# Softmax groups of eight heads instead of four, with the loads of keys and values reshaped to match, in a decode transformer block

## The chip, the cores and the metric

The kernel runs on 1 core of one Trainium2 chip. The metric is device time in microseconds (us) for one execution. The kernel before takes 189.02 us, the median of 3 runs (188.81 to 189.14).

## The reference

One decode step of a transformer block with adaptive layer norm, batch 2, one query token per batch entry. Attention over the last 1024 of 4096 cached tokens, then a gated FFN. Cut to the attention:

```python
B, Sq, D = 2, 1, 640
Hq = Hkv = 32; Sk = 4096; Dh = 192
W = 1024                                  # min(4096, max(256, Sk // 4))
q = (h @ wq).reshape(B, Sq, Hq, Dh).transpose(0, 2, 1, 3)
k = k_cache[:, :, Sk - W:, :]             # (B, 32, 1024, 192) bfloat16
v = v_cache[:, :, Sk - W:, :]
p = softmax(einsum('bhqd,bhkd->bhqk', q, k) * Dh ** -0.5)
o = einsum('bhqk,bhkd->bhqd', p, v)       # then @ wo, residual, layer norm, FFN
```

Keys and values are 50.3 MB of the 76.9 MB that have to be read (2 tensors x 2 batch entries x 32 heads x 1024 tokens x 192 x 2 bytes). The weights are the rest.

## The kernel before

K and V, the keys and values, are read from off-chip memory (HBM; the page counts 76.88 MB read from it) and pass through a ring of 8 slots in on-chip memory (SBUF, 128 partitions or "rows"). A slot holds one load: one contiguous run of 12288 B for each of the 128 rows, 1.57 MB. A group is four heads of one batch entry. Row 4p + i of a slot holds 32 neighbouring tokens, block p of 32, of head i of 4. DVE (VectorE) multiplies K by the query, PE (TensorE, the matmul engine) adds up over part of the head dimension, DVE finishes the scores, and one softmax chain per group follows (maximum, subtract, exp on ACT, which is ScalarE, denominator, probabilities times V or "PV", scaling).

```python
HQ = 4                      # heads in a group
PH = P // HQ                # 32 token blocks
J = W // PH                 # 32 tokens in each row
NG = B * NQD                # 16 groups
NS, SLOT = 8, J * Dh        # ring
# ... order of the loads: wq, k0, then k(g) and v(g-1) in turn, then wo
def ring_src(it):
    # ... wq and wo cut
    quad, b = group(i)
    src = A_k_cache if kind == "k" else A_v_cache
    return src[b].rearrange("(i u) s d -> u i s d", u=NQD)[quad, :, K0:Sk, :].rearrange("i (p j) d -> p i (j d)", p=PH), SLOT
# ... one DMA for each load, issued as soon as the slot's last user is known
S.dma("sp", k_dma(ring_f[:, o0:o0 + width], src), sem_ring[slot_of[it]], writes=ring_key(it), ...)
```

What the DMA instruction gets from this, in elements (step, count), outermost dimension first: source `[6144, 32] [6291456, 4] [1, 6144]`, destination `[49152, 128] [1, 1] [1, 6144]`. The text calls this shape 32 x 4: 32 blocks of 4 runs.

Of the kernel before, what the change touches and what calls it, by code (L numbers as in the profile page):

```python
# [5 lines left out]
ALU = mybir.AluOpType  # L6
ACTF = mybir.ActivationFunctionType
AX = mybir.AxisListType
BF16 = mybir.dt.bfloat16
# [110 lines left out]
def bass_adaLN_cond__sliding_block_cached__geglu_ffn__decode_kernel(  # L120
# [14 lines left out]
    P = 128  # L135
    B, _, D = A_x.shape
    _, H, Sk, Dh = A_k_cache.shape
    F = B_w_gate.shape[1]
    W = min(4096, max(256, Sk // 4))
    K0 = Sk - W  # L140
    KT = D // P
    NQ = H * Dh
    NR = 4
    DR = D // NR
    HQ = 4
    PH = P // HQ
    J = W // PH
    NQD = H // HQ
    NG = B * NQD
    NT = NQ // P  # L150
    DD = Dh // NT
# [3 lines left out]
    assert DD * NT == Dh and DD * H == P and NR * FR == FC and FC * P == F and DR == KT * 32  # L155
    assert HQ == NR and DD * NQD == 32
    SCALE = float(Dh) ** -0.5
    EPS = 1e-5
    NEG = 1e30
    JC = 16  # L160
    NCK = J // JC
    GC = 512 // JC
    NCH = Dh // GC
    assert GC * NCH == Dh and NCK == 2
    ON = 2 * Dh
    NPAIR = J // 2

    NS = 8
    SLOT = J * Dh
    WQ_SPLIT = [(0, 2), (2, 3)]  # L170
# [6 lines left out]
    HP = P // 2  # L177
    X0 = DD * NQD - 1
    ZW = X0 + P
    QW = 512  # L180
    NQB = NQ // (NR * QW)
    FT = F // NR
    assert NQB * QW == NQD * Dh
    MH = 3 * DR

    es = ExitStack()
    with es:
# [23 lines left out]
        selrow = sb("selrow", [P, NR, B], BF16)  # L211
        selq = sb("selq", [P, B, P], BF16)
        ztmp = sb("ztmp", [P, NR, 2, HQ], BF16)
# [39 lines left out]
        def bank(k):  # L253
            return ("bank", k)
# [13 lines left out]
        items = [("wq", k) for k in range(NWQ)]  # L268
        items += [("k", 0)]
        for g in range(1, NG):  # L270
            items += [("k", g), ("v", g - 1)]
        items += [("v", NG - 1)]
        items += [("wo", i) for i in range(NWO)]
# [18 lines left out]
        def group(g):  # L292
            return divmod(g, B)

        def ring_src(it):
            kind, i = it
            if kind == "wq":
                k0, n = WQ_SPLIT[i]
                return A_wq.rearrange("(p k) n -> p (k n)", k=KT)[:, k0 * NQ:(k0 + n) * NQ], n * NQ
            if kind == "wo":  # L300
                t0, n = WO_SPLIT[i]
                return A_wo.rearrange("(p t) n -> p (t n)", t=NT)[:, t0 * D:(t0 + n) * D], n * D
            quad, b = group(i)
            src = A_k_cache if kind == "k" else A_v_cache
            return src[b].rearrange("(i u) s d -> u i s d", u=NQD)[quad, :, K0:Sk, :].rearrange("i (p j) d -> p i (j d)", p=PH), SLOT

# [17 lines left out]
        for nm, t in (("scT", scT), ("oT", oT), ("aT", aT)):  # L324
# [15 lines left out]
                                                compare_op=ALU.is_equal, fill=0.0, base=0, channel_multiplier=1),  # L340
             reads=["ones_b"], writes=["selg"], name="selg")
        for b in range(B):
            S.op("pool", lambda e, b=b: e.affine_select(out=selq[:, b, :].rearrange("p (x h) -> p x h", h=HQ),
                                                        in_=ones_b[:, 0:1].unsqueeze(2).broadcast_to([P, PH, HQ]),
                                                        pattern=[[0, PH], [-32, HQ]],
                                                        compare_op=ALU.is_equal, fill=0.0, base=-b, channel_multiplier=1),
                 reads=["ones_b"], writes=[("selq", b)], name="selq%d" % b)
        S.op("pool", lambda e: e.affine_select(out=ztmp[:, :, :, :].rearrange("p i q h -> p i (q h)"),
# [61 lines left out]
        def ln_mod(tag, opc_idx, s_idx, dst_bf):  # L410
# [7 lines left out]
            def f(e):  # L418
                last = None
                hv = hrow[:, :].rearrange("p (m j) -> p m j", j=KT)  # L420
                for j in range(KT):
                    for i in range(NR):
# [10 lines left out]
             reads=["mask_h"], writes=["maskc"], name="maskc")  # L433
        S.op("dve", lambda e: e.tensor_reduce(out=zsel[:, :, X0:X0 + P].rearrange("p q (h m) -> p q h m", m=32)[:, :, :, 0],
                                              in_=ztmp[:, :, :, :].rearrange("p i q h -> p q h i"), axis=AX.X, op=ALU.max),
# [36 lines left out]
        for n in range(NQB):  # L472
# [3 lines left out]
            else:  # L476
                S.op("dve", lambda e, n=n: e.tensor_copy(out=qrow[:, n * QW:(n + 1) * QW], in_=ps[:, n, :]),  # L477
                     reads=[bank(n)], writes=[("qrow", n)], name="q1_evac%d" % n)
        for u, (n, b) in enumerate((n, b) for n in range(NQB) for b in range(B)):
            bk = BK_T + u % 4  # L480
            S.op("pe", lambda e, n=n, b=b, bk=bk: e.matmul(ps[:, bk, :], lhsT=selq[:, b, :], rhs=qrow[:, n * QW:(n + 1) * QW], start=True, stop=True),
                 reads=[("selq", b), ("qrow", n)], writes=[bank(bk)], name="q2_%d_%d" % (n, b))
            S.op("act", lambda e, n=n, b=b, bk=bk: e.activation(out=qbc[:, b, n * QW:(n + 1) * QW], in_=ps[:, bk, :], func=ACTF.Copy),  # L483
                 reads=[bank(bk)], writes=[("qbc", b, n)], name="q2_evac%d_%d" % (n, b))
        S.op("dve", lambda e: e.memset(ps[:, 5:8, :], 0.0), writes=[bank(k) for k in range(5, 8)], name="init_O2")  # L485

        def d_mul(g, ci):
            quad, b = group(g)
            sl = slot_of[("k", g)]
            S.op("dve", lambda e: e.tensor_tensor(out=prod[:, 2 * (g % 2) + ci, :, :],  # L490
                                                  in0=ring[:, sl, ci * JC * Dh:(ci + 1) * JC * Dh].rearrange("p (j d) -> p j d", d=Dh),
                                                  in1=qbc[:, b, quad * Dh:(quad + 1) * Dh].unsqueeze(1).broadcast_to([P, JC, Dh]), op=ALU.mult),
                 reads=[("ring", sl)] + [("qbc", b, n) for n in range(quad * Dh // QW, ((quad + 1) * Dh - 1) // QW + 1)], writes=[("prod", 2 * (g % 2) + ci)], name="mul%d_%d" % (g, ci))

        def p_reduce(g, ci):
            pz = 2 * (g % 2) + ci

            def f(e):
                last = None
                o_ap = ps[:, pz, :].rearrange("p (j c) -> p j c", c=GC)  # L500
                for t in range(NCH):
                    last = e.matmul(o_ap, lhsT=ident_b[:, :], rhs=prod[:, pz, :, t * GC:(t + 1) * GC],  # L502
                                    start=(t == 0), stop=(t == NCH - 1))
                return last
            S.op("pe", f, reads=[("prod", pz), "ident_b"], writes=[bank(pz)], name="red%d_%d" % (g, ci))

        def c_sum(g):
            z = g % 2
            S.op("dve", lambda e: e.tensor_reduce(out=S_sb[:, z, :], in_=ps[:, 2 * z:2 * z + 2, :].rearrange("p k (j c) -> p (k j) c", c=GC),  # L509
                                                  axis=AX.X, op=ALU.add),  # L510
                 reads=[bank(2 * z), bank(2 * z + 1)], writes=[("S", z)], name="sum_%d" % g)
            S.op("dve", lambda e: e.tensor_reduce(out=M1[:, z:z + 1], in_=S_sb[:, z, :], axis=AX.X, op=ALU.max),  # L512
                 reads=[("S", z)], writes=[("M1", z)], name="max_%d" % g)
            S.op("pe", lambda e: e.transpose(ps[0:1, BK_T, 0:P], M1[:, z:z + 1], ident_f[:, :]),
                 reads=[("M1", z), "ident_f"], writes=[bank(BK_T)], name="T_%d" % g)
# [26 lines left out]

        def p_pv(g):
            z = g % 2
            sl = slot_of[("v", g)]

            def f(e):
                last = None
                for jp in range(NPAIR):
                    i = jp % NR  # L550
                    last = e.matmul(ps[32 * i:32 * i + 2 * HQ, BK_O, 0:ON],  # L551
                                    lhsT=E_sb[:, z, 2 * jp:2 * jp + 2, :].rearrange("p j h -> p (j h)"),
                                    rhs=ring[:, sl, 2 * jp * Dh:(2 * jp + 2) * Dh],
                                    start=(jp < NR), stop=(jp >= NPAIR - NR), tile_position=(0, 32 * i))
                return last
            S.op("pe", f, reads=[("E", z), ("ring", sl)], writes=[bank(BK_O)], name="PV_%d" % g)

# [24 lines left out]

        for g in range(NG + 2):
            has = g < NG
            prev = 1 <= g <= NG
            pp = g >= 2
            if has:
                d_mul(g, 0)
                p_reduce(g, 0)
            if pp:  # L590
                c_rec(g - 2)
            if prev:
                c_sum(g - 1)
            if has:
                d_mul(g, 1)
                declare_ring([("k", g)])
            if prev:
                c_max2(g - 1)
                c_bc(g - 1)
            if has:  # L600
                p_reduce(g, 1)
            if prev:
                c_exp(g - 1)
                p_den(g - 1)
            if pp:
                p_sel(g - 2)
            if prev:
                p_pv(g - 1)
                declare_ring([("v", g - 1)])

# [119 lines left out]
```

## Time and profile before

| | before |
|---|---|
| time, median | 189.02 us |
| DMA rate, 60 to 140 us | 426 GB/s |
| DVE busy, PE busy, ACT busy | 98.2, 107.5, 29.9 us of a span of 187.6 |
| end of the last weight load | 184.4 us |

The first part of the page to read is the span in 40 slices. DMA is the mean busy share of the 16 DMA engines in tenths, and GB/s is what they moved:

```profile
DVE  6131100019588988886595695775865933003211
...
DMA  7999998999999999999999999999999999999991
GB/s 254 402 451 435 430 459 372 422 435 424 430 422 422 427 425 426 427 424 420 419 432 432 422 423 422 421 438 422 424 423 422 419 488 428 416 384 442 398 396 45
```

DMA is at 9 (90% or more) nearly from end to end, and after the start the rate is mostly between 415 and 440 GB/s. DVE has gaps. The same for one stretch (the last two columns are the DMA share and GB/s):

```profile
core 0: us, PE busy (x) PEld busy (x) DVE busy (x) ACT busy (x) POOL busy (x), PEclk, DMA share, GB/s
60.00:140.00 80.00, 54.89 (x440) 27.29 (x439) 61.19 (x83) 11.42 (x36) 0.00 (x0) 0.96 1.01 426
```

The list of DMA issues gives the kind of load, the count, the size and the median time from issue to landing:

```profile
ring<-in_A_k_cache_dram SPq DMA_DIRECT2D x16, 1536.0 KB, 24.4
ring<-in_A_v_cache_dram SPq DMA_DIRECT2D x16, 1536.0 KB, 24.2
```

One load takes 3.7 us at 426 GB/s, so 24 us mean that six or seven loads are queued. Last, what the main DVE step waited for (waits of all engines):

```profile
engine line waited for: us in total, times, longest us
...
DVE prod L490 <- DMA ring<-in_A_k_cache_dram: 14.3, 9, 1.6
```

The products wait 14.3 us in all for K. The kernel is bound by its loads. The chain that ended last says the same, in shares of the span by engine:

```profile
## 4 chain that ended last, share of the span: by engine, by line
DMA 71%; DVE 15%; PE 7%; ACT 2%; SPq 2%; issue 1%
```

### The profile page before, as it was taken

To read this page: it belongs to the slowest core of one execution; us is meant where nothing else is said; L and a number is where in the kernel's file an instruction comes from. 1 tells how busy PE (TensorE), PEld (TensorE's weight loads), DVE (VectorE), ACT (ScalarE), POOL (GpSimd) and SP (SyncE) were. 2 spreads that over 40 slices of the span, in tenths; PEclk is the share of its full clock that TensorE was granted. 3 is DMA by queue.
4 is the path that set the end of the run, shared out by engine and by line. 5 is a ranking of instruction groups with operands and counts; after the bars stand their busy time and mean duration, and the time that the engine had idled before them with its cause. 6 is when DMAs were issued, how large, how long until landed. Compare 5 with 4: busy or idle time off the path is not lost.

```text
span 187.6 us, 2409 instructions
## 1 busy us (share of the span) xinstructions
PE 107.5 (57%) x1039; PEld 51.1 (27%) x1039; DVE 98.2 (52%) x147; ACT 29.9 (16%) x72; POOL 5.1 (3%) x23
## 2 busy tenths in 40 slices
PE   0014730742968887676676655675497395364462
PEld 0011200210323443333423323233253152353121
DVE  6131100019588988886595695775865933003211
ACT  3041100082001221112011110210120103103400
POOL 8200000000000000000000000000000000000000
PEclk9999999997587999999879999999969967569696
DMA  7999998999999999999999999999999999999991
GB/s 254 402 451 435 430 459 372 422 435 424 430 422 422 427 425 426 427 424 420 419 432 432 422 423 422 421 438 422 424 423 422 419 488 428 416 384 442 398 396 45
DMA packets 6518, 77.03 MB, mean 411 GB/s; under 512 B 746, under 2 KB 876, under 8 KB 1516
## 3 DMA queue, kind: packets, MB, share of 16 engines
q1 hardware_dynamic: 6492, 76.88, 97.1%
q8 instruction: 8, 0.13, 0.3%
q10 hardware_dynamic: 16, 0.01, 0.0%
q14 instruction: 2, 0.02, 0.0%
HBM read 76.88 MB, written 0.00 MB: 410 GB/s over the span
## 4 chain that ended last, share of the span: by engine, by line
DMA 71%; DVE 15%; PE 7%; ACT 2%; SPq 2%; issue 1%
DMA ring<-in_A_k_cache_dram 37%; DMA ring<-in_A_wq_dram 17%; DMA r<-in_B_w_down_dram 17%; DVE prod L490 9%; PE ps L502 4%; DVE S_sb L509 4%; PE ps L467 2%; SPq L266 2%; ACT qbc L483 2%; DVE ps L485 1%; DVE M L512 1%; ACT qrow L474 1%; PE ps L526 0%; DVE bcR L519 0%; PE ps L684 0%
## 5 line engine op out<-in xcount | busy, mean ns | idle before, releaser
L490 DVE TENSOR_TENSOR prod<-ring,qbc 128x3072 bf16<-128x3072 bf16 x32 | 55.9, 1751 | 14.3 <-DMA ring<-in_A_k_cache_dram 14.3
L502 PE MATMUL ps<-prod,ident_b 128*128 128x512 bf16 x192 | 52.9, 419 | 14.4 <-DVE prod L490 14.4
L502 PEld LDWEIGHTS ps<-prod,ident_b 128*128 128x128 bf16 x192 | 17.5, 104 | 40.2 <-DVE prod L490 17.5
L509 DVE TENSOR_REDUCE S_sb<-ps 128x32 f32<-128x1024 f32 x16 | 19.3, 1206 | 2.1 <-PE ps L502 2.1
L526 PE MATMUL ps<-bcR,bcL 5*128 5x4 f32 x32 | 6.1, 258 | 21.9 <-DVE bcR L519 21.9
L563 ACT ACTIVATE On<-ps,rden 128x384 bf16<-128x384 f32 x16 | 9.3, 580 | 43.5 <-DVE rden L561 21.1
L551 PE MATMUL ps<-ring,E_sb 128*8 128x384 bf16 x256 | 15.5, 369 | 0.0
L534 ACT ACTIVATE E_sb<-Sb_sb 128x128 bf16<-128x128 f32 x16 | 5.0, 310 | 56.4 <-DVE Sb_sb L531 56.4
L467 PE MATMUL ps<-ring,hT 128*2 128x512 bf16 x60 | 6.7, 626 | 9.8 <-DMA ring<-in_A_wq_dram 8.8
L526 PEld LDWEIGHTS ps<-bcR,bcL 5*128 5x128 f32 x32 | 4.7, 183 | 26.1 <-DVE bcR L519 26.1
L477 DVE CAST qrow<-ps 128x512 bf16<-128x512 f32 x1 | 0.7, 692 | 15.7 <-PE ps L467 15.7
L622 PE MATMUL ps<-ring,oT 128*17 128x160 bf16 x192 | 5.5, 294 | 5.6 <-DMA ring<-in_A_wo_dram 5.6
L531 DVE TENSOR_TENSOR Sb_sb<-S_sb,ps 128x128 f32<-128x128 f32 x16 | 4.6, 287 | 7.6 <-PE ps L526 7.6
L540 PEld LDWEIGHTS ps<-denp,maskc 128*128 128x128 f32 x32 | 7.1, 224 | 3.7 <-ACT E_sb L534 0.9
L641 DVE TENSOR_TENSOR lnt<-ps,modR 128x160 f32<-128x160 f32 x1 | 0.3, 325 | 12.6 <-PE ps L622 12.6
L445 PE MATMUL ps<-r,scT 128*17 128x480 bf16 x40 | 4.3, 597 | 3.9 <-DMA r<-in_w_mod_dram 3.9
L622 PEld LDWEIGHTS ps<-ring,oT 128*17 128x17 bf16 x192 | 4.9, 117 | 6.2 <-DMA ring<-in_A_wo_dram 6.2
L551 PEld LDWEIGHTS ps<-ring,E_sb 128*8 128x8 bf16 x256 | 5.1, 90 | 3.7 <-issue 1.2
L396 PE MATMUL ps<-st,selstat 128*128 128x2 f32 x4 | 0.9, 298 | 8.6 <-ACT sqj L392 8.6
L467 PEld LDWEIGHTS ps<-ring,hT 128*2 128x2 bf16 x60 | 1.7, 114 | 14.7 <-DMA ring<-in_A_wq_dram 9.7
L576 PE MATMUL ps<-On,zsel 128*128 128x96 bf16 x64 | 5.2, 241 | 0.7 <-ACT On L563 0.7
L540 PE MATMUL ps<-denp,maskc 128*128 128x1 f32 x32 | 5.1, 230 | 0.8 <-ACT E_sb L534 0.8
(81 smaller groups left out, 71.2 us busy)
## 6 DMA issues: line engine op xcount, KB each, us to landing
ring<-in_A_k_cache_dram SPq DMA_DIRECT2D x16, 1536.0 KB, 24.4
ring<-in_A_v_cache_dram SPq DMA_DIRECT2D x16, 1536.0 KB, 24.2
r<-in_w_mod_dram SPq DMA_DIRECT2D x1, 4800.0 KB, 14.3
ring<-in_A_wq_dram SPq DMA_DIRECT2D x1, 4608.0 KB, 32.3
ring<-in_A_wo_dram SPq DMA_DIRECT2D x1, 4480.0 KB, 23.4
ring<-in_A_wq_dram SPq DMA_DIRECT2D x1, 3072.0 KB, 21.2
ring<-in_A_wo_dram SPq DMA_DIRECT2D x1, 2720.0 KB, 24.1
r<-in_B_w_gate_dram SPq DMA_DIRECT2D x1, 1920.0 KB, 25.0
```

Source lines behind the costliest of these rows:

```text
L467: last = e.matmul(ps[32 * i:32 * i + B, n, :], lhsT=hT[:, k, :], rhs=wv[:, kk, i, n * QW:(n + 1) * QW], start=(k == 0), stop=(k == KT - 1) ...
L490: S.op("dve", lambda e: e.tensor_tensor(out=prod[:, 2 * (g % 2) + ci, :, :], in0=ring[:, sl, ci * JC * Dh:(ci + 1) * JC * Dh].rearrange("p ...
L502: last = e.matmul(o_ap, lhsT=ident_b[:, :], rhs=prod[:, pz, :, t * GC:(t + 1) * GC], start=(t == 0), stop=(t == NCH - 1))
L509: S.op("dve", lambda e: e.tensor_reduce(out=S_sb[:, z, :], in_=ps[:, 2 * z:2 * z + 2, :].rearrange("p k (j c) -> p (k j) c", c=GC), axis=A ...
L526: S.op("pe", lambda e: e.matmul(ps[:, BK_T, P:P + HQ], lhsT=bcL[:, :], rhs=bcR[:, z, :], start=True, stop=True), reads=[("bcR", z), "bcL"] ...
L531: S.op("dve", lambda e: e.tensor_tensor(out=Sb_sb[:, z, :, :], in0=S_sb[:, z, :].unsqueeze(2).broadcast_to([P, J, HQ]), in1=ps[:, BK_T, P: ...
L534: S.op("act", lambda e: e.activation(out=E_sb[:, z, :, :], in_=Sb_sb[:, z, :, :], func=ACTF.Exp, scale=SCALE, accum_out=denp[:, z:z + 1]), ...
L540: S.op("pe", lambda e: e.matmul(ps[:, BK_T, P + 16:P + 17], lhsT=maskc[:, :], rhs=denp[:, z:z + 1], start=True, stop=True), reads=[("denp" ...
L551: last = e.matmul(ps[32 * i:32 * i + 2 * HQ, BK_O, 0:ON], lhsT=E_sb[:, z, 2 * jp:2 * jp + 2, :].rearrange("p j h -> p (j h)"), rhs=ring[:, ...
L563: S.op("act", lambda e: e.activation(out=On[:, quad % 2, b, :], in_=ps[:, BK_O, 0:ON], func=ACTF.Identity, scale=rden[:, z:z + 1]), reads= ...
L576: last = e.matmul(ps[:, BK_OT, 0:B * NT].rearrange("p (b t) -> p b t", b=B), lhsT=zsel[:, jj, x:x + P], rhs=On[:, quad % 2, :, jj * Dh + d ...
L622: last = e.matmul(ps[32 * i:32 * i + RM, BK_M, 0:DR], lhsT=oT[:, t, :], rhs=wv[:, tl, i, :], start=(t == 0), stop=(t == NT - 1), tile_posi ...
```

## The change

Its intent is to halve the number of softmax chains: groups of eight heads, 8 groups instead of 16. Eight heads on 128 rows leave 16 token blocks of 64 tokens. So that a slot keeps its size, each K or V of a group comes as two loads, each with half of every block's 64 tokens.

```diff
-    HQ = 4
+    HQ = 8
+    V = HQ // NR
+    JS = 32
+    NSUB = J // JS
...
-    SLOT = J * Dh
+    SLOT = JS * Dh
...
-        items += [("k", 0)]
-        for g in range(1, NG):
-            items += [("k", g), ("v", g - 1)]
-        items += [("v", NG - 1)]
+        items += [("k", sq) for sq in range(NSUB)]
+        for sq in range(NSUB, NG * NSUB):
+            items += [("k", sq), ("v", sq - NSUB)]
+        items += [("v", sq) for sq in range((NG - 1) * NSUB, NG * NSUB)]
...
-            return src[b].rearrange("(i u) s d -> u i s d", u=NQD)[quad, :, K0:Sk, :].rearrange("i (p j) d -> p i (j d)", p=PH), SLOT
+            g, sub = divmod(i, NSUB)
+            quad, b = group(g)
+            return src[b].rearrange("(h u) s d -> u h s d", u=NQD)[quad, :, K0:Sk, :].rearrange("h (x s j) d -> s x h (j d)", x=PH, s=NSUB)[sub], SLOT
...
# cut: the query is spread to eight heads by two matmuls and four evictions; products, partial sums
# and PV go by half runs; maximum, subtract, exp, denominator and scaling go once for each group of eight
```

The DMA instruction now gets the source `[12288, 16] [3145728, 8] [1, 6144]` and the same destination: 128 runs of 12288 B as before.

More of the change, by code (lines that the diff above doesn't have):

```diff
@@ L155, in bass_adaLN_cond__sliding_block_cached__geglu_ffn__decode_kernel @@
     assert DD * NT == Dh and DD * H == P and NR * FR == FC and FC * P == F and DR == KT * 32
-    assert HQ == NR and DD * NQD == 32
+    assert V * NR == HQ and JS * NSUB == J and 2 * HQ <= 32
     SCALE = float(Dh) ** -0.5
@@ L160, in bass_adaLN_cond__sliding_block_cached__geglu_ffn__decode_kernel @@
     JC = 16
-    NCK = J // JC
+    NCK = JS // JC
     GC = 512 // JC
@@ L165, in bass_adaLN_cond__sliding_block_cached__geglu_ffn__decode_kernel @@
     ON = 2 * Dh
-    NPAIR = J // 2
+    NPAIR = JS // 2
     NS = 8
-    SLOT = J * Dh
+    SLOT = JS * Dh
     WQ_SPLIT = [(0, 2), (2, 3)]
@@ L177, in bass_adaLN_cond__sliding_block_cached__geglu_ffn__decode_kernel @@
     HP = P // 2
-    X0 = DD * NQD - 1
+    HS = DD * NQD
+    X0 = HS - 1
     ZW = X0 + P
@@ L182, in bass_adaLN_cond__sliding_block_cached__geglu_ffn__decode_kernel @@
     FT = F // NR
-    assert NQB * QW == NQD * Dh
+    UW = min(2, NQD)
+    QU = UW * Dh
+    NQU = NQD // UW
+    assert NQB * QW == NQ // NR == V * NQD * Dh
     MH = 3 * DR
@@ L211, in bass_adaLN_cond__sliding_block_cached__geglu_ffn__decode_kernel @@
         selrow = sb("selrow", [P, NR, B], BF16)
-        selq = sb("selq", [P, B, P], BF16)
+        selq = sb("selq", [P, B, V, P], BF16)
         ztmp = sb("ztmp", [P, NR, 2, HQ], BF16)
@@ L302, in ring_src @@
                 return A_wo.rearrange("(p t) n -> p (t n)", t=NT)[:, t0 * D:(t0 + n) * D], n * D
-            quad, b = group(i)
+            g, sub = divmod(i, NSUB)
+            quad, b = group(g)
             src = A_k_cache if kind == "k" else A_v_cache
-            return src[b].rearrange("(i u) s d -> u i s d", u=NQD)[quad, :, K0:Sk, :].rearrange("i (p j) d -> p i (j d)", p=PH), SLOT
+            return src[b].rearrange("(h u) s d -> u h s d", u=NQD)[quad, :, K0:Sk, :].rearrange("h (x s j) d -> s x h (j d)", x=PH, s=NSUB)[sub], SLOT
         def declare_ring(consumed=()):
@@ L341, in bass_adaLN_cond__sliding_block_cached__geglu_ffn__decode_kernel @@
              reads=["ones_b"], writes=["selg"], name="selg")
+        S.op("pool", lambda e: e.memset(selq[:, :, :, :], 0.0), writes=["selq"], name="selq0")
         for b in range(B):
-            S.op("pool", lambda e, b=b: e.affine_select(out=selq[:, b, :].rearrange("p (x h) -> p x h", h=HQ),
-                                                        in_=ones_b[:, 0:1].unsqueeze(2).broadcast_to([P, PH, HQ]),
-                                                        pattern=[[0, PH], [-32, HQ]],
-                                                        compare_op=ALU.is_equal, fill=0.0, base=-b, channel_multiplier=1),
-                 reads=["ones_b"], writes=[("selq", b)], name="selq%d" % b)
+            for v in range(V):
+                S.op("pool", lambda e, b=b, v=v: e.affine_select(out=selq[:, b, v, :].rearrange("p (x i v) -> p x i v", i=NR, v=V)[:, :, :, v],
+                                                                 in_=ones_b[:, 0:1].unsqueeze(2).broadcast_to([P, PH, NR]),
+                                                                 pattern=[[0, PH], [-32, NR]],
+                                                                 compare_op=ALU.is_equal, fill=0.0, base=-b, channel_multiplier=1),
+                     reads=["ones_b"], writes=["selq"], name="selq%d_%d" % (b, v))
         S.op("pool", lambda e: e.affine_select(out=ztmp[:, :, :, :].rearrange("p i q h -> p i (q h)"),
@@ L433, in bass_adaLN_cond__sliding_block_cached__geglu_ffn__decode_kernel @@
              reads=["mask_h"], writes=["maskc"], name="maskc")
-        S.op("dve", lambda e: e.tensor_reduce(out=zsel[:, :, X0:X0 + P].rearrange("p q (h m) -> p q h m", m=32)[:, :, :, 0],
+        S.op("dve", lambda e: e.tensor_reduce(out=zsel[:, :, X0:X0 + P].rearrange("p q (h m) -> p q h m", m=HS)[:, :, :, 0],
                                               in_=ztmp[:, :, :, :].rearrange("p i q h -> p q h i"), axis=AX.X, op=ALU.max),
@@ L478, in bass_adaLN_cond__sliding_block_cached__geglu_ffn__decode_kernel, with f @@
                      reads=[bank(n)], writes=[("qrow", n)], name="q1_evac%d" % n)
-        for u, (n, b) in enumerate((n, b) for n in range(NQB) for b in range(B)):
-            bk = BK_T + u % 4
-            S.op("pe", lambda e, n=n, b=b, bk=bk: e.matmul(ps[:, bk, :], lhsT=selq[:, b, :], rhs=qrow[:, n * QW:(n + 1) * QW], start=True, stop=True),
-                 reads=[("selq", b), ("qrow", n)], writes=[bank(bk)], name="q2_%d_%d" % (n, b))
-            S.op("act", lambda e, n=n, b=b, bk=bk: e.activation(out=qbc[:, b, n * QW:(n + 1) * QW], in_=ps[:, bk, :], func=ACTF.Copy),
+        for z, (n, b) in enumerate((n, b) for n in range(NQU) for b in range(B)):
+            bk = BK_T + z % 4
+            def f(e, n=n, b=b, bk=bk):
+                last = None
+                for v in range(V):
+                    o0 = NQD * Dh * v + n * QU
+                    last = e.matmul(ps[:, bk, 0:QU], lhsT=selq[:, b, v, :], rhs=qrow[:, o0:o0 + QU], start=(v == 0), stop=(v == V - 1))
+                return last
+            S.op("pe", f, reads=["selq"] + [("qrow", m) for m in range(NQB)], writes=[bank(bk)], name="q2_%d_%d" % (n, b))
+            S.op("act", lambda e, n=n, b=b, bk=bk: e.activation(out=qbc[:, b, n * QU:(n + 1) * QU], in_=ps[:, bk, 0:QU], func=ACTF.Copy),
@@ L484, in bass_adaLN_cond__sliding_block_cached__geglu_ffn__decode_kernel, with d_mul @@
                  reads=[bank(bk)], writes=[("qbc", b, n)], name="q2_evac%d_%d" % (n, b))
         S.op("dve", lambda e: e.memset(ps[:, 5:8, :], 0.0), writes=[bank(k) for k in range(5, 8)], name="init_O2")
-        def d_mul(g, ci):
-            quad, b = group(g)
-            sl = slot_of[("k", g)]
-            S.op("dve", lambda e: e.tensor_tensor(out=prod[:, 2 * (g % 2) + ci, :, :],
+        def d_mul(sq, ci):
+            quad, b = group(sq // NSUB)
+            sl = slot_of[("k", sq)]
+            pz = 2 * (sq % 2) + ci
+            S.op("dve", lambda e: e.tensor_tensor(out=prod[:, pz, :, :],
@@ L491, in d_mul @@
                                                   in0=ring[:, sl, ci * JC * Dh:(ci + 1) * JC * Dh].rearrange("p (j d) -> p j d", d=Dh),
                                                   in1=qbc[:, b, quad * Dh:(quad + 1) * Dh].unsqueeze(1).broadcast_to([P, JC, Dh]), op=ALU.mult),
-                 reads=[("ring", sl)] + [("qbc", b, n) for n in range(quad * Dh // QW, ((quad + 1) * Dh - 1) // QW + 1)], writes=[("prod", 2 * (g % 2) + ci)], name="mul%d_%d" % (g, ci))
-        def p_reduce(g, ci):
-            pz = 2 * (g % 2) + ci
+                 reads=[("ring", sl), ("qbc", b, quad // UW)], writes=[("prod", pz)], name="mul%d_%d" % (sq, ci))
@@ L498, in f, with p_reduce @@
+        def p_reduce(sq, ci):
+            pz = 2 * (sq % 2) + ci
             def f(e):
@@ L504, in f, with c_sum, c_max @@
                 return last
-            S.op("pe", f, reads=[("prod", pz), "ident_b"], writes=[bank(pz)], name="red%d_%d" % (g, ci))
-        def c_sum(g):
+            S.op("pe", f, reads=[("prod", pz), "ident_b"], writes=[bank(pz)], name="red%d_%d" % (sq, ci))
+        def c_sum(sq):
+            g, sub = divmod(sq, NSUB)
+            z, w = g % 2, sq % 2
+            S.op("dve", lambda e: e.tensor_reduce(out=S_sb[:, z, sub * JS:(sub + 1) * JS], in_=ps[:, 2 * w:2 * w + 2, :].rearrange("p k (j c) -> p (k j) c", c=GC),
+                                                  axis=AX.X, op=ALU.add),
+                 reads=[bank(2 * w), bank(2 * w + 1)], writes=[("S", z)], name="sum_%d" % sq)
+        def c_max(g):
             z = g % 2
-            S.op("dve", lambda e: e.tensor_reduce(out=S_sb[:, z, :], in_=ps[:, 2 * z:2 * z + 2, :].rearrange("p k (j c) -> p (k j) c", c=GC),
-                                                  axis=AX.X, op=ALU.add),
-                 reads=[bank(2 * z), bank(2 * z + 1)], writes=[("S", z)], name="sum_%d" % g)
             S.op("dve", lambda e: e.tensor_reduce(out=M1[:, z:z + 1], in_=S_sb[:, z, :], axis=AX.X, op=ALU.max),
@@ L541, in p_den, with p_pv @@
                  reads=[("denp", z), "maskc"], writes=[bank(BK_T)], name="den_%d" % g)
-        def p_pv(g):
+        def p_pv(sq):
+            g, sub = divmod(sq, NSUB)
             z = g % 2
-            sl = slot_of[("v", g)]
+            sl = slot_of[("v", sq)]
             def f(e):
@@ L550, in f @@
                     i = jp % NR
+                    j0 = sub * JS + 2 * jp
                     last = e.matmul(ps[32 * i:32 * i + 2 * HQ, BK_O, 0:ON],
-                                    lhsT=E_sb[:, z, 2 * jp:2 * jp + 2, :].rearrange("p j h -> p (j h)"),
+                                    lhsT=E_sb[:, z, j0:j0 + 2, :].rearrange("p j h -> p (j h)"),
                                     rhs=ring[:, sl, 2 * jp * Dh:(2 * jp + 2) * Dh],
-                                    start=(jp < NR), stop=(jp >= NPAIR - NR), tile_position=(0, 32 * i))
+                                    start=(sub == 0 and jp < NR), stop=(sub == NSUB - 1 and jp >= NPAIR - NR), tile_position=(0, 32 * i))
                 return last
-            S.op("pe", f, reads=[("E", z), ("ring", sl)], writes=[bank(BK_O)], name="PV_%d" % g)
+            S.op("pe", f, reads=[("E", z), ("ring", sl)], writes=[bank(BK_O)], name="PV_%d" % sq)
         def c_rec(g):
@@ L581, in p_sel @@
             S.op("pe", f, reads=[("On", quad % 2, bb) for bb in range(B)] + ["zsel"], writes=[bank(BK_OT)], name="sel_%d" % quad)
-        for g in range(NG + 2):
+        for sq in range((NG + 1) * NSUB + 1):
+            g, sub = divmod(sq, NSUB)
             has = g < NG
             prev = 1 <= g <= NG
-            pp = g >= 2
+            head = sub == 0
+            pp = g >= 2 and head
             if has:
-                d_mul(g, 0)
-                p_reduce(g, 0)
+                d_mul(sq, 0)
+                p_reduce(sq, 0)
             if pp:
                 c_rec(g - 2)
-            if prev:
-                c_sum(g - 1)
+            if 1 <= sq <= NG * NSUB:
+                c_sum(sq - 1)
+            if prev and head:
+                c_max(g - 1)
             if has:
-                d_mul(g, 1)
-                declare_ring([("k", g)])
-            if prev:
+                d_mul(sq, 1)
+                declare_ring([("k", sq)])
+            if prev and head:
                 c_max2(g - 1)
@@ L600, in bass_adaLN_cond__sliding_block_cached__geglu_ffn__decode_kernel @@
             if has:
-                p_reduce(g, 1)
-            if prev:
+                p_reduce(sq, 1)
+            if prev and head:
                 c_exp(g - 1)
@@ L607, in bass_adaLN_cond__sliding_block_cached__geglu_ffn__decode_kernel @@
             if prev:
-                p_pv(g - 1)
-                declare_ring([("v", g - 1)])
+                p_pv(sq - NSUB)
+                declare_ring([("v", sq - NSUB)])
         S.op("act", lambda e: e.activation(out=oT[:, :, 0:RM:RB].rearrange("p t b -> p b t"),
```

## The prediction

> **What bounds the kernel now.** The loads. The page's 40 slices show the DMA engines at 99% busy in nearly every slice, and the table of stretches gives 423 to 427 GB/s from 17 to 145 us (share 0.98 to 1.01). [...] 76.88 MB have to come in, and the order of loads ends with w_down, whose last piece lands at 184.4 us; only 3.2 us follow (last down matmuls, two DVE steps, the store). Compute has room: DVE 52%, PE 57% of the span.
>
> The queue is deep. The list of DMA issues shows a K or V load taking 24 us from issue to landing, while one load of 1.57 MB needs 3.7 us at 425 GB/s: six to seven loads wait ahead of each. A slot could come free 20 us later.
>
> **What the change removes (groups by form, times of before).** Groups go from 16 to 8.
> - DVE: the 32 products (1751 ns) and 16 sums (1206 ns) stay. Per group there are now max 186, max over blocks 272, subtract 287, reciprocal 162 ns, 14.5 us in all. After: the subtract has 512 columns instead of 128, estimated 690 ns; max about 220; so 8 x 1.34 = 10.7 us. DVE saves about 4 us of 98.
> - ACT: 8 of 16 output scalings (580 ns) go, 4.6 us; exp becomes 8 x about 600 ns, no gain.
> - PE: 8 transposes, 8 broadcasts, 8 denominators (near 0.3 to 0.4 us each), and 32 of 64 selection matmuls: 8 to 11 us.
> - Query broadcast: four evictions of 384 columns instead of six of 512, but each waits for all of qrow; the first product starts perhaps 0.5 us earlier.
>
> **What it moves.** Loads keep number (32), size and the contiguous run of 12288 B; only the addresses differ (16 blocks x 8 heads, runs 24576 B apart instead of adjacent). V lags K by two loads instead of one, but each turn still consumes one K and one V, so ring occupancy is the same. The last wo piece and the FFN weights behind it now wait for a V slot instead of the last K's; that is perhaps 2 to 4 us later than 150 us, with the two earlier wo pieces landing until 169.6 us: hidden.
>
> **On the critical path: about nothing.** All that is saved is compute under a full DMA queue. The bytes, their rate and the tail stay.
>
> **Predicted: 188.9 us, 80% range 187.9 to 190.3.** Faster by over 2%: 0.03; within 2%: 0.92; slower: 0.05.
>
> **What would show it.** DMA slices still 99% and 420 to 427 GB/s from 17 to 145 us; landing time of K and V still 22 to 26 us; DVE busy about 94 us, ACT about 24, PE about 98; chain of waits still ending in w_down landing at 184 us, tail 3 us.
>
> **What would make it wrong.** A change in load rate from the new address pattern: [...] heads are 6 MB apart now against 12 MB. No run here shows such a loss; weights (other row lengths) and K/V run at the same 423 to 427. Second, a group's chain now holding two V slots longer, draining the queue: landing times would fall well below 20 us and DMA slices drop.

The forecast adds up to 188.9 us: the 189 us of before, less almost nothing, because the loads end at 184.4 us and 3.2 us follow. The rate that the argument rests on is the measured one, 423 to 427 GB/s from 17 to 145 us. The fear of the new addresses is a guess of mine.

Three times in it are estimates, and the groups of the kernel before lead to them. The subtract: 287 ns for 128 columns (L531) and 557 for 384 of another TENSOR_TENSOR (L664), on one line, give 692 for 512. The maximum: 186 ns for 32 columns (L512) and 320 for 160 of another reduction (L394) give 220 for 64. The exp: near the 615 ns of another ACT operation on 512 columns (L483). The kernel after took 687, 220 and 629 ns. The 0.5 us of the query broadcast and the 2 to 4 us of the last loads are guesses, and neither enters the sum.

## The result, and the profile after

The kernel after takes 298.87 us, the median of 4 runs (295.76 to 301.25). Two of them count as fast (295.76 and 297.15) and two as slow (300.58 and 301.25). The ratio to before is 1.568, 95% interval 1.562 to 1.575. Ratios are the mean time of one kernel's fast runs over that of the other's of the same rounds, so not quite the ratio of the medians that are quoted. The profiled run is a fast one (297.15 us).

The slices of the kernel after:

```profile
DVE  5210017653333415260606070516233354100031
...
DMA  8999999999999999999999999999999999999993
GB/s 328 401 443 442 278 221 215 228 221 216 225 220 220 225 226 223 225 220 223 227 215 230 221 223 228 218 230 221 233 226 228 226 236 230 235 424 405 417 412 144
```

The busy share of the DMA engines is what it was: 9 nearly throughout. The rate is not. It is above 400 GB/s while weights come in (the second to fourth slice, and four near the end), and 215 to 236 GB/s for the 30 slices of K and V. The stretch from 60 to 140 us:

```profile
60.00:140.00 80.00, 35.01 (x189) 12.44 (x186) 28.21 (x28) 3.33 (x8) 0.00 (x0) 0.70 1.01 222
```

The share is 1.01 both times, and the rate fell from 426 to 222 GB/s. The issues of the kernel after:

```profile
ring<-in_A_k_cache_dram SPq DMA_DIRECT2D x16, 1536.0 KB, 51.4
ring<-in_A_v_cache_dram SPq DMA_DIRECT2D x16, 1536.0 KB, 53.5
```

The queue did not run dry. It got slower: 51 us to landing instead of 24 for the same queue of same-sized loads. The waits of the products on K:

```profile
engine line waited for: us in total, times, longest us
...
DVE prod L507 <- DMA ring<-in_A_k_cache_dram: 114.8, 15, 9.6
```

From 14.3 to 114.8 us: DVE now stands and waits. The added wait of 100.5 us is close to the added span of 107.8 us.

The chain that ended last has to be read with care here:

```profile
## 4 chain that ended last, share of the span: by engine, by line
DMA 41%; another core or an unknown queue 31%; DVE 21%; PE 4%; SPq 2%; issue 1%
```

There is only one core, so "another core or an unknown queue" is something that the chain could not name. The timeline names it. Start, duration, engine, line and operation, and in brackets the idle time before, with what ended it:

```profile
85.79 1.76 DVE L507 TENSOR_TENSOR prod<-ring,qbc 128x3072 bf16<-128x3072 bf16 x1 [9.63 <-DMA ring<-in_A_k_cache_dram]
...
99.92 1.76 DVE L507 TENSOR_TENSOR prod<-ring,qbc 128x3072 bf16<-128x3072 bf16 x1 [7.67 <-DMA ring<-in_A_k_cache_dram]
...
114.04 1.76 DVE L507 TENSOR_TENSOR prod<-ring,qbc 128x3072 bf16<-128x3072 bf16 x1 [9.57 <-DMA ring<-in_A_k_cache_dram]
```

In this window the chain has two pieces without a name, which end at 99.9 and 114.0 us. At both a product starts that waited for K.

The trace also has each DMA packet with its size and duration. The run of 12288 B is one packet, and there are 4096 of them in both kernels (count, duration in ns):

```
before  12288 B  n=4096  mean 464  p10 460  median 464  p90 468
after   12288 B  n=4096  mean 882  p10 755  median 920  p90 949
```

So number and size of these packets are unchanged, all 16 engines are occupied (share 1.01), and the typical packet takes 920 ns instead of 464, 1.98 times as long. The 128 packets of 24576 B of a weight load did not change (912 ns in both).

### The profile page after: what moved, and what is told of

Read it like the earlier page. It is cut to its first block, busy times and chain, and to the rows that moved or that the text cites. A ratio compares the mean times of both kernels' runs of the same rounds, so it can differ in the third digit from the quotient of the medians.

```text
span 295.4 us, 2209 instructions
## 1 busy us (share of the span) xinstructions
PE 127.3 (43%) x969; PEld 50.7 (17%) x969; DVE 96.2 (33%) x115; ACT 23.2 (8%) x46; POOL 5.9 (2%) x26
## 4 chain that ended last, share of the span: by engine, by line
DMA 41%; another core or an unknown queue 31%; DVE 21%; PE 4%; SPq 2%; issue 1%
DMA ring<-in_A_k_cache_dram 15%; DVE prod L507 14%; DMA r<-in_B_w_down_dram 14%; DMA ring<-in_A_wq_dram 12%; DVE S_sb L527 5%; SPq L273 2%; DVE Sb_sb L552 1%; PE ps L477 1%; PE ps L547 1%; PE ps L519 1%; DVE bcR L540 0%; DVE M L533 0%; PE ps L574 0%; PE ps L711 0%
## 5 line engine op out<-in xcount | busy, mean ns | idle before, releaser
L519 PE MATMUL ps<-prod,ident_b 128*128 128x512 bf16 x192 | 74.9, 553 | 102.9 <-DVE prod L507 102.4
L507 DVE TENSOR_TENSOR prod<-ring,qbc 128x3072 bf16<-128x3072 bf16 x32 | 56.0, 1752 | 114.8 <-DMA ring<-in_A_k_cache_dram 114.8
L519 PEld LDWEIGHTS ps<-prod,ident_b 128*128 128x128 bf16 x192 | 21.6, 126 | 147.1 <-DVE prod L507 116.5
L574 PE MATMUL ps<-ring,E_sb 128*16 128x384 bf16 x256 | 16.0, 380 | 10.7 <-DMA ring<-in_A_v_cache_dram 10.7
L586 ACT ACTIVATE On<-ps,rden 128x384 bf16<-128x384 f32 x8 | 4.6, 581 | 163.5 <-DVE rden L584 137.1
L574 PEld LDWEIGHTS ps<-ring,E_sb 128*16 128x16 bf16 x256 | 5.4, 96 | 19.1 <-DMA ring<-in_A_v_cache_dram 15.4
L555 ACT ACTIVATE E_sb<-Sb_sb 128x512 bf16<-128x512 f32 x8 | 5.0, 629 | 44.0 <-DVE Sb_sb L552 44.0
L552 DVE TENSOR_TENSOR Sb_sb<-S_sb,ps 128x512 f32<-128x512 f32 x8 | 5.5, 687 | 4.7 <-PE ps L547 4.7
L547 PE MATMUL ps<-bcR,bcL 9*128 9x8 f32 x16 | 4.0, 318 | 4.2 <-DVE bcR L540 4.2
L547 PEld LDWEIGHTS ps<-bcR,bcL 9*128 9x128 f32 x16 | 3.2, 249 | 8.9 <-DVE bcR L540 8.9
L682 PE MATMUL ps<-r,h2T 128*2 128x384 bf16 x40 | 3.8, 505 | 0.5 <-DVE h2T L437 0.3
```

Of the source, the lines that this page charges most:

```text
L507: S.op("dve", lambda e: e.tensor_tensor(out=prod[:, pz, :, :], in0=ring[:, sl, ci * JC * Dh:(ci + 1) * JC * Dh].rearrange("p (j d) -> p j ...
L519: last = e.matmul(o_ap, lhsT=ident_b[:, :], rhs=prod[:, pz, :, t * GC:(t + 1) * GC], start=(t == 0), stop=(t == NCH - 1))
L547: S.op("pe", lambda e: e.matmul(ps[:, BK_T, P:P + HQ], lhsT=bcL[:, :], rhs=bcR[:, z, :], start=True, stop=True), reads=[("bcR", z), "bcL"] ...
L552: S.op("dve", lambda e: e.tensor_tensor(out=Sb_sb[:, z, :, :], in0=S_sb[:, z, :].unsqueeze(2).broadcast_to([P, J, HQ]), in1=ps[:, BK_T, P: ...
L555: S.op("act", lambda e: e.activation(out=E_sb[:, z, :, :], in_=Sb_sb[:, z, :, :], func=ACTF.Exp, scale=SCALE, accum_out=denp[:, z:z + 1]), ...
L574: last = e.matmul(ps[32 * i:32 * i + 2 * HQ, BK_O, 0:ON], lhsT=E_sb[:, z, j0:j0 + 2, :].rearrange("p j h -> p (j h)"), rhs=ring[:, sl, 2 * ...
```

## The experiments

Three questions were put in turn. Is it the loads, or what is computed? If the loads: their addresses in HBM, or the shape in which they are written? If the shape: by what mechanism? Kernels called wrong on purpose read other data than they should. They still pass the comparison with the reference, whose tolerance does not notice which cache entries are averaged, so passing says little about attention in any run here. All outputs passed. In the expectations, the shape theory is that the shape of the loads makes them slow, the phase theory that the loss comes from DMA engines that go through their runs in step (see below). Where only one run was made, its state is unknown; the differences read from such runs are many times the spread of the kernel after (295.76 to 301.25).

### The new loads in the old kernel

```diff
 # kernel before
-            return src[b].rearrange("(i u) s d -> u i s d", ...)   # 32 x 4 runs
+            g8, sub = divmod(i, 2)
+            quad, b = divmod(g8, B)
+            return src[b].rearrange("(h u) s d -> u h s d", u=4)[quad, :, K0:Sk, :].rearrange("h (x s j) d -> s x h (j d)", x=16, s=2)[sub], SLOT
```

> The kernel before, computing as before, with the loads of K and V of the kernel after (wrong result on purpose). Load theory (the new loads alone are slow, whatever is computed): about 298 us, K/V stretch at 220 to 230 GB/s. Compute theory (groups of eight heads hold slots longer or drain the queue): 189 us, 425 GB/s.

Measured: 299.19 us (one run; the kernel before 188.94). The stretch from 60 to 140 us:

```profile
60.00:140.00 80.00, 40.08 (x198) 16.47 (x187) 30.56 (x40) 5.50 (x16) 0.00 (x0) 0.63 1.01 220
```

The new loads alone are the whole loss. Groups of eight heads are not needed for it.

### The old loads in the new kernel

```diff
 # kernel after
-            return src[b].rearrange("(h u) s d -> u h s d", ...)   # 16 x 8 half runs
+            quad, b = divmod(i, B)
+            return src[b].rearrange("(i u) s d -> u i s d", u=8)[quad, :, K0:Sk, :].rearrange("i (p j) d -> p i (j d)", p=32), SLOT
```

> The kernel after, computing as after, with the loads of K and V of the kernel before (wrong result on purpose). Load theory: 189 us within 1%, 425 GB/s, and the time left is what the groups of eight heads alone are worth: my prediction said about nothing (188.9). Compute theory: about 298 us.

Measured: 189.15 us, median of 6 runs (188.79 to 189.48), ratio to before 1.0008 (0.9993 to 1.0023).

```profile
60.00:140.00 80.00, 55.96 (x367) 22.52 (x360) 58.58 (x59) 7.10 (x16) 0.00 (x0) 0.86 1.01 425
```

Without the new loads nothing is lost, and nothing is gained: eight chains instead of sixteen are worth nothing measurable here. The busy times did fall, from 98.2 to 95.8 us on DVE, 29.9 to 23.2 on ACT and 107.5 to 105.2 on PE, under DMA engines that are occupied (share 1.01 in the stretch).

### The new shape, other addresses

```diff
 # kernel after: 16 x 8 runs, but the eight runs are neighbours in HBM
+            t0 = (quad * NSUB + sub) * 8192
+            return src[b].rearrange("h s d -> (h s) d")[t0:t0 + 16 * 264, :].rearrange("(x r) d -> x (r d)", x=PH)[:, 0:HQ * SLOT].rearrange("x (h n) -> x h n", h=HQ), SLOT
```

> The kernel after, each load still written as 16 x 8 runs of 12288 B into the same partitions, but the 8 runs lie next to each other in HBM and the 16 are 101 KB apart, all in one stretch of 1.6 MB (wrong result on purpose). Shape theory [...]: stays near 298 us, 220 to 230 GB/s. Address theory (spacing in HBM is what slows the reads): back to about 189 us.

Measured: 298.99 us.

```profile
60.00:140.00 80.00, 38.33 (x191) 14.03 (x191) 29.08 (x29) 3.33 (x8) 0.00 (x0) 0.66 1.01 222
```

### The old shape, the new spacing

```diff
 # kernel before: 32 x 4 runs, but 24576 B apart, and heads 6 MB apart
+            return src[b].rearrange("(w i u) s d -> w u i s d", w=2, u=4)[quad // 4, quad % 4, :, Sk - 2 * W:Sk, :].rearrange("i (p s j) d -> s p i (j d)", p=PH, s=2)[b], SLOT
```

> The kernel before, each load still written as 32 x 4 runs of 12288 B, but with the spacing of the kernel after: runs 24576 B apart, heads 6 MB apart (wrong result on purpose). Shape theory: stays at 189 us, 425 GB/s. Address theory: slows to about 298 us.

Measured: 188.91 us. Packets of 12288 B took 464 ns, as before.

```profile
60.00:140.00 80.00, 55.16 (x439) 27.27 (x440) 60.42 (x81) 11.61 (x36) 0.00 (x0) 0.96 1.01 425
```

These two close the question of addresses. Reads from one compact stretch of HBM are slow when written as 16 x 8 (222 GB/s), and reads with the spacing of the kernel after are fast when written as 32 x 4 (425 GB/s).

### Whole runs instead of half runs

In the change each K or V of a group comes as two loads, each with half of every block. This kernel keeps groups of eight heads and loads each K or V at once, in pairs of slots, and is meant to be right.

```diff
 # kernel after
+        nslots.update({(kv, g): NSUB for kv in "kv" for g in range(NG)})
+            return src[b].rearrange("(h u) s d -> u h s d", u=NQD)[quad, :, K0:Sk, :].rearrange("h (x j) d -> x h (j d)", x=PH), NSUB * SLOT
 # cut: order of items, release of both slots after the second half; wo in pieces of 19, 28 and 1
```

> The kernel after, correct, groups of eight heads, but each K and V in one load of whole runs of 24576 B (16 x 8, pairs of ring slots) in place of two half-run loads. Shape and phase theories: still slow, about 298 us, because the outermost count is still 16. If the halving of the runs is the cause: about 189 us.

Measured: 308.19 us.

```profile
60.00:140.00 80.00, 32.07 (x161) 12.22 (x165) 31.62 (x30) 3.33 (x8) 0.00 (x0) 0.70 1.00 213
```

Halving the runs is not the cause. K and V now come in packets of 24576 B, which take 1893 ns in the median, against 912 ns for the packets of the same size of a weight load with 128 outermost rows in the same run.

### What the shape does: a theory

What the runs so far show is 213 to 222 GB/s with 16 x 8 in place of 425 to 426, and packets of 12288 B that take 920 ns instead of 464, with the same bytes into the same 128 rows. They do not show why. The following is a guess of mine.

With 16 source blocks and 16 DMA engines, suppose that each engine takes one block. It would then write that block's eight neighbouring rows one after the other. If all engines go through their eight runs in step, they might get in each other's way, and that might be why a packet takes twice as long. The trace has no engine number for a packet, and nothing in it shows where in SBUF the writes would meet, so both the split and the collision are assumed. So is the split of 32 x 4: if an engine took two neighbouring blocks of four rows there, it would write the same eight rows in the same order, and by this theory the kernel before would be slow too. If the theory holds, its 426 GB/s need another split, and no run shows why the two shapes are split differently. What can be tested is a consequence: the loss should depend on the engines being in step.

### Engines put out of step

Two small loads ahead of the first K, with outermost counts of 12 and 4. The intent was that each of them occupies only a part of the engines, so that the engines come to the first K at different times. The increments of their semaphores, 13 and 5 against 16 for a load of K or V (see below), fit 12 and 4 engines; which ones, the trace does not show.

```diff
 # kernel after, before the load of k0 (n = 4; also n = 8 and n = 2)
+    for sm, k, o in ((sem_sk[0], 12, 0), (sem_sk[1], 4, SLOT)):
+        S.dma("sp", k_dma(pf[0:k * n, o:o + SLOT], <k x n runs of 12288 B>), sm, writes=[("prod", ...)])
```

> The kernel after, correct, its 32 loads untouched; two small extra loads ahead of the first K load, one with an outermost count of 12 and one of 4 (four runs of 12288 B for each count, 0.79 MB together)[...]. Phase theory [...]: [...] 190 to 196 us, K/V at 400 GB/s or more, packets of 12288 B back near 464 ns. If [...] writing eight neighbouring partitions is slow in itself: 298 to 302 us, because 0.79 MB were added.

Measured: 230.14 us, median of 4 runs (223.52 to 234.35). One of them, the fastest, counts as fast; the rest differ from it by over 1.5% and count as slow, the profiled one (234.35) too. All lie 60 us and more under the kernel after; fast against fast it is 223.52 against 295.76 and 297.15.

```profile
60.00:140.00 80.00, 46.44 (x259) 16.80 (x259) 45.50 (x44) 5.21 (x12) 0.00 (x0) 0.81 1.01 332
```

> The same with eight runs for each count (1.57 MB extra): engines out of step by eight runs, a full turn[...]. Phase theory: slow as the kernel after, 298 to 305 us, though the extra loads and the unevenness are twice those of the skew by four. A theory in which unevenness between engines as such helps: as fast as the skew by four.

Measured: 305.45 us.

```profile
60.00:140.00 80.00, 38.56 (x179) 13.85 (x178) 33.10 (x31) 3.33 (x8) 0.00 (x0) 0.67 1.01 227
```

> The same with two runs for each count: engines out of step by two of eight runs. Phase theory, estimate: [...] 290 GB/s, about 245 us; between 225 and 265. Other theories: 298 us.

Measured: 279.04 us, outside the range of 225 to 265; 253 to 289 GB/s in most later slices of K and V. The 290 GB/s that were expected were an estimate of mine, and it rested on the assumed collision. 50.3 MB at 290 GB/s are 174 us, and the kernel before has 71 us beside its K and V (189 less 118 at 426 GB/s), 245 us together. The stretch:

```profile
60.00:140.00 80.00, 32.49 (x191) 11.71 (x191) 30.90 (x30) 3.33 (x8) 0.00 (x0) 0.78 1.01 237
```

Reading the three together: adding 0.79 MB of loads made the kernel some 70 us faster, adding 1.57 MB of the same made it 6.6 us slower than the kernel after (1.57 MB take 7 us at 222 GB/s), and half of the small dose gave a part. So neither unevenness nor bytes are what helps; an offset within eight runs fits all three. The 332 GB/s also speak against a theory in which writing eight neighbouring rows is slow in itself, as K and V were written just as in the kernel after. Two things came out worse than expected: a skew by four gave 332 GB/s and not 400, and a skew by two 237 and not 290.

I suspected that the extra loads themselves collided with K and V and blurred the skew. So I moved them: the runs of count 12 from the first 48 rows to rows 4 and 5 of the first 12 blocks of eight, those of count 4 from the first 16 rows to rows 6 and 7 of the first four blocks (for a skew by two, to row 4 and to row 5). That these rows avoid a collision was assumed; no run shows it:

```diff
 # kernel after, before the load of k0: n loads with count 12 and n with count 4 (n = 4; also n = 2)
+    for q in range(2 * n):
+        k, r0, o = (12 if q < n else 4), 4 + q // 2, (q % 2) * SLOT
+        S.dma("sp", k_dma(pf[r0:r0 + 8 * (k - 1) + 1:8, o:o + SLOT], <k runs of 12288 B>), sem_sk[q], writes=[("skew", q)])
 # the first products wait for these loads
```

> The skew by four again (230 us before, less recovery than I expected)[...]. If the missing part of the recovery came from a skew blurred by collisions of the extra loads, now 190 to 205 us and at least 390 GB/s in the K/V stretch. If skews are not held as engines drift, or the phase explains only a part: 220 to 240 us as before.

Measured: 234.64 us, median of 4 runs (223.73 to 240.16), 323 GB/s in the stretch of the profiled run (a slow one, 238.80 us). It missed the 390 GB/s: the other placement brought nothing.

> The same with a skew by two of eight runs. Phase theory[...]: 235 to 280 us, between the clean skew by four and the kernel after. Otherwise 298 us.

Measured: 269.93 us, 273 GB/s: within the range, between the skew by four and none.

The packets of the profiled run of the kernel with the clean skew by four (start in us from the first packet, 12288 B packets only):

```
60 to 80 us    n=559  mean 579 ns
80 to 100 us   n=565  mean 564 ns
100 to 120 us  n=502  mean 644 ns
180 to 200 us  n=540  mean 595 ns
```

The mean never gets to 464 ns and wanders, while in the kernel after it stays at 861 to 895 ns in every 20 us. I took that for engines that drift against each other once they are out of step. It was not tested further, and the skew is not offered as a cure.

The trace holds more, which no view of the profile prints: the time of each semaphore increment with which a load reports that it has landed.

- Every load of K or V leaves 16 increments, which would fit one for each of the 16 engines. The extra load of count 12 left 13 (one at 3.5 us, the other twelve from 36.0 to 40.9 us), the one of count 4 left 5, which would fit 12 and 4 engines.
- In the kernel after, from 60 to 140 us, 14 of the 16 increments of a load come within 0.9 to 1.5 us, while a load takes 7.1 us. I read that as nearly all engines in step. By the same reading they are in step in the kernel before (0.5 to 1.7 of 3.7 us), which runs at 426 GB/s.
- With the skew by eight most come in three bunches about one load apart (near 61, 67.5 and 74 us for one load). With the skew by four the first K load shows bunches of 4, 7 and 5 some 2.6 us apart, and by 116 us they are spread over 10 us without bunches.

By this reading the skews were put in place, and the engines do drift. But drift does not account for what is missing: with the bunches still clear, the first loads after the skew by four took 5.1 to 5.3 us each (about 300 GB/s), and later ones, less bunched, mostly 4.5 to 4.9. By the phase theory the first ones should have gone at the full rate, 3.7 us. At best the theory explains a part of the loss, and what the rest is stays open.

### The same source, other rows

The most direct test of the written side: each K or V as eight loads of one head. The two kernels differ in nothing but the rows that head h goes to.

```diff
 # kernel after, each load of K or V
+    for h in range(HQ):
+        last = e.dma_start(ring_f[h:P:HQ, o0:o0 + SLOT], src[:, h, :])              # first kernel: rows h, h+8, ...
+        last = e.dma_start(ring_f[PH * h:PH * h + PH, o0:o0 + SLOT], src[:, h, :])  # second kernel: rows 16h to 16h+15
```

> The kernel after, correct, each load of K or V as eight loads of one head each: 16 runs into rows h, h+8, h+16 and so on. [...] as the kernel after, 295 to 305 us; it is also the control for what eight times as many loads cost.

Measured: 298.54 us.

```profile
60.00:140.00 80.00, 36.14 (x191) 13.05 (x191) 29.68 (x29) 3.33 (x8) 0.00 (x0) 0.72 1.02 223
```

> The same eight loads of one head each with the same source, but head h goes into the 16 neighbouring rows 16h to 16h+15 (wrong result on purpose)[...]: half of the rate again, about 112 GB/s in the K/V stretch, packets of 12288 B near 1.85 us, and about 450 us for 50.3 MB plus 70 us for the rest, so 480 to 540 us. If [...] the shape of the source decides: as the control, about 298 us.

Measured: 379.86 us, outside the range of 480 to 540. The slices of this kernel:

```profile
GB/s 325 441 454 230 132 138 134 138 135 135 145 145 146 145 145 150 160 156 157 160 155 173 173 170 174 175 171 183 180 186 184 191 195 201 209 224 383 411 418 213
```

With the same source and the same number of loads, other destination rows cost 81 us more. So the rows written change the rate: 142 GB/s in the stretch with 16 neighbouring rows at a time, 223 with 16 rows eight apart. The direction is the expected one, the size missed. The 112 GB/s were half of the rate of the kernel after; why it should halve again was an assumption of mine. The other outcome, as the control, would have meant that the shape of the source decides. The rate starts at 132 to 138 GB/s, somewhat above the expected 112, and climbs to 224; packets go from 1451 ns at 60 to 100 us to 964 at 320 to 340. That here too the engines fall out of step in time is a guess; why the rate climbs was not shown.

### All runs

| kernel | shape of K and V loads | us | GB/s, 60 to 140 us |
|---|---|---|---|
| before | 32 x 4 | 189.02 | 426 |
| after, old loads | 32 x 4 | 189.15 | 425 |
| before, new spacing | 32 x 4 | 188.91 | 425 |
| after | 16 x 8 | 298.87 | 222 |
| before, new loads | 16 x 8 | 299.19 | 220 |
| after, compact addresses | 16 x 8 | 298.99 | 222 |
| after, whole runs | 16 x 8 | 308.19 | 213 |
| after, eight loads, rows 8 apart | 8 times 16 | 298.54 | 223 |
| after, eight loads, neighbouring rows | 8 times 16 | 379.86 | 142 |
| after, skew 8 of 8 | 16 x 8 | 305.45 | 227 |
| after, skew 2, clean skew 2 | 16 x 8 | 279.04, 269.93 | 237, 273 |
| after, skew 4, clean skew 4 | 16 x 8 | 230.14, 234.64 | 332, 323 |

## Why the prediction was wrong

- **What bounds the kernel, and where the tail ends: right.** The loads bind, before and after. The weights at the end run at 384 GB/s or more in both, the last slice aside.
- **What the groups of eight remove: right in effect, too high in size for DVE and PE.** The new kernel with the old loads took 189.15 us against 188.9 predicted. DVE fell by 2.4 us (about 4 predicted), ACT by 6.7 (about 6, from 29.9 to 24), PE by 2.3 (8 to 11 predicted). A part of PE's shortfall goes with the granted clock: the 192 partial-sum matmuls, the same in both, took 433 ns each at 0.844 in that profile against 419 at 0.901 (and 553 at 0.713 in the kernel after), which is 2.2 us of busy time (55.1 against 52.9). None of it was on the critical path.
- **The step that failed: "The bytes, their rate and the tail stay", resting on "only the addresses differ".** Bytes, count and run length stayed. The rate of K and V went from 426 to 222 GB/s, because the loads were written as 16 x 8 instead of 32 x 4. At these rates 50.3 MB take 227 us instead of 118, which is 109 us, and the kernel lost 110.
- **The risk was named at the wrong end.** The prediction feared the addresses in HBM. Both tests of that came out against it (298.99 us with compact addresses, 188.91 us with the new spacing). What changed was the shape in which the rows are written (222 GB/s as 16 x 8, 426 as 32 x 4); that this regroups the rows over the engines is a guess. The destination pattern looks the same in both instructions, so the difference is easy to miss. It was there to be read in the diff: 32 blocks became 16.
- **The reading of "weights and K/V run at the same 423 to 427" was too wide.** It showed only that row length did not matter among those loads. All of them had an outermost count of 128 or 32, and none had 16.
- **Two of the signs said nothing.** "DMA slices still 99%" came true at half the rate (the slices say only 90% or more, the stretch 1.01). The other, landing times well below 20 us, would have meant a dry queue; they rose to 51 us instead.

Shown: the new loads are the whole loss (299.19 us in the old kernel); addresses and half runs are not the cause (298.99 and 308.19 us without them); the shape is (188.91 to 189.15 us as 32 x 4); with one and the same source, the rows written change the rate (142 against 223 GB/s); the extra loads of four runs give a part back (332 GB/s) and those of eight give nothing (227). Assumed: which engine writes which row, in 32 x 4 as in 16 x 8, and that writes of engines in step collide. Not shown: where they would collide. Open: why a skew of half a turn recovers about half of the lost rate and not all, even before the engines drift.

## What to carry to other kernels

A DMA that moved the same bytes in the same runs into the same rows ran here at half the rate (222 against 426 GB/s) because of how its outermost dimension is counted, so look at the counts of a changed load, not only at size and addresses: here 32 outermost blocks or 128 rows were fast, and 16 blocks of eight rows were not. The busy share of the DMA engines was 1.01 at both rates: it says that they are occupied, not how fast they move data; read GB/s and the duration of one packet of known size (464 against 920 ns) beside it. And the savings in compute under a full DMA queue were worth nothing measurable here (189.15 us), while the change of layout that feeds that queue cost 110 us.
